# Sparse attention feeding a gated layer: another first stage, another load order

## The chip, the cores and the metric

The kernel runs on one core of a Trainium2 chip. A core has five engines with instruction streams of their own: TensorE (PE, matrix products and transposes into PSUM), VectorE (DVE), ScalarE (ACT), GpSimd (POOL) and SyncE (SP, which here only issues transfers). They meet through semaphores, and each works through its own instructions strictly in order: an instruction that waits holds up all that stand behind it on its engine. Sixteen DMA engines move data between device memory and SBUF. SP, ACT and POOL issue transfers on a queue each (q1, q10 and q0 in the profile). The metric is the device time of one execution in microseconds.

## The reference

Inputs are q, k, v of shape (4, 8, 768, 64), and the weights of a gated layer, w_gate and w_val (512 x 1536) and w_out (1536 x 512).

```
ub[t, c]  = sum over d of max(q[t,d] * kmin[c,d], q[t,d] * kmax[c,d])   # per head; chunks of 32 keys
top       = the 6 chunks with the largest ub, of those not ahead of t's own chunk
scores    = q @ k.T / 8, only where the chunk is in top and the key isn't ahead of t
attn      = softmax(scores)
x         = attn @ v, the heads side by side           # 3072 x 512
out       = (sigmoid(x @ w_gate) * (x @ w_val)) @ w_out
```

The first 128 rows of a sequence have at most four chunks, so there all causal chunks are selected. For the others the selection has to be made. The bound is written as a product: max(q kmin, q kmax) = q kmin + max(q, 0) (kmax - kmin), so that queries and their rectified copy, one below the other in 128 partitions, meet key minima and ranges (kcat) in a single product.

## The kernel before

The work is cut into nine stages. Batch 0 starts with stages of 128 rows (stage 0), 256 rows (stage 1) and 384 rows (stage 2), and the other three batches are two stages of 384 rows each. Every stage has a preparation (queries and keys transposed so that head_dim lies in the partitions; chunk minima and maxima; bounds; selection), the attention (scores, exponentials, product with the values, normalization, transposition to xT), and the gated layer (products with w_gate and w_val called gv, tanh called gate, hglu, and the output product o).

The order of all instructions is written out by hand in a list, ORDER: one name per operation, kind:stage.count, with /1 or /2 for the second or third engine that may do it. The class Plan resolves the names and emits the operations in that order; each engine gets those of its own in the order of the list. Plan also has estimated times, from which it decides only where TensorE gets filler products (fill, line 340: products of zeros, up to 36 us of its estimate) so that its clock stays up while it waits. It knows only the waits of its estimate. PSUM has two large accumulators of two banks ("big") and four small ones of one bank ("m"), handed out in turn: a new one waits until the fourth one before it has been read.

Stage 0 has a form of its own. Keys and queries come as 128 x 512 blocks (first_loads, _groups), are transposed by four fp32 products each (line 561) and evicted from PSUM: keys into firstK, queries raw and rectified into first (evict_queries, line 522, four times on ACT). From the bounds (L699) it takes a guard, a number for each query and head that is subtracted from its scores so that the exponential stays in range (L704 to L708). The guard is transposed and copied into eight extra rows of first (L712), and firstK has minus one there, so that a single product of 72 rows gives guarded scores (L810). After the exponential (L815), GpSimd zeroes what lies ahead of the diagonal (L821). Then the product with the values (L835) and the normalization (L846, L848).

Stages 1 and 2 are made by prep_groups too. They transpose into the large accumulators and evict the queries twice for each half of the partitions, raw and rectified (L522 on ACT, L526 on VectorE): eight evictions in stage 1, twelve in stage 2. Chunk minima and maxima are L571, the key block kcat L580 to L591, key evictions L604, the cast of the queries to 16 bit L537. L733 is the bounds' product, L736 to L757 the selection, L761 its copies into the query block, L810 the scores, L891 the gated layer's products, L901 and L903 its gate, L917 the output product.

Stage 0's values arrive in two halves of 128 KB, one on SP's queue and one on ACT's, are then cast to 16 bit by GpSimd (L491). On ACT's queue the order of issue is stage 0's queries, stage 1's first values (256 KB), stage 0's second half of values. GpSimd issues the weights (w0 to w8, L507 and L509) between the constants that it builds.

## Time and profile before

| | us |
|---|---|
| median of 3 runs | 300.29 |
| lowest and highest | 300.08, 301.04 |
| the profiled execution | 300.8 |
| its span, first to last instruction | 298.8 |
| TensorE busy | 284.5 |
| VectorE, ScalarE, GpSimd busy | 212.4, 203.9, 107.5 |
| filler products on TensorE | 11.2 |
| moved by DMA | 27.99 MB |

Times in the views count from the span's first instruction. In the rows of stretches, behind the length stand the busy time of each engine with the number of its instructions (TensorE, its weight loads, VectorE, ScalarE, GpSimd), then the granted TensorE clock, the mean share of the DMA engines in use, and GB/s. In the rows of the timeline stand start, duration, engine, line, operation, output and inputs; in brackets the idle time ahead of it and what ended that. In the rows of a line, behind the number of instructions stand their shortest, median and longest duration in ns, and the first and last start. In the DMA queues' rows stand packets, MB, and the time that the packets took as a share of 16 engines' time.

### The profile page before, as it was taken

The numbers are of one execution on the slowest core, as the hardware profiler recorded it, in microseconds if no ns is written. First come the engines' busy times: TensorE is split into PE (matmuls) and PEld (weight loads), VectorE is DVE, ScalarE is ACT, GpSimd is POOL, SyncE is SP. The second block draws the span as 40 slices with busy tenths as digits, with TensorE's granted clock in tenths as the row PEclk, the third lists the DMA queues.
The fourth block names the chain that finished last, engine by engine and source line by source line (L and its number), as shares of the span: only waits on it lengthen the run. The fifth ranks groups of instructions, "written<-read, shape, count | busy, mean of one in ns | idle before, by whom it ended". The sixth has DMA issues, their size and how long they took to land.

```text
span 298.8 us, 6823 instructions
## 1 busy us (share of the span) xinstructions
PE 284.5 (95%) x2642; PEld 181.2 (61%) x2642; DVE 212.4 (71%) x581; ACT 203.9 (68%) x299; POOL 107.5 (36%) x175
## 2 busy tenths in 40 slices
PE   6668998999999999999999999999999999999995
PEld 3345983865665566566655656766665676555563
DVE  0688788998999898899988886897875434202431
ACT  3578896899786598887995886999636476331221
POOL 7567703685568143273851104326220101000000
PEclk9999999999999999999999999999999999999999
DMA  7999999999699273575790500006210000021012
GB/s 152 256 218 279 229 171 114 193 149 175 74 215 160 43 141 58 96 63 109 111 85 2 124 0 2 3 3 71 20 70 2 35 2 0 2 103 39 0 70 106
DMA packets 110072, 27.99 MB, mean 94 GB/s; under 512 B 100311, under 2 KB 105525, under 8 KB 110040
## 3 DMA queue, kind: packets, MB, share of 16 engines
q1 hardware_dynamic: 81608, 19.28, 31.5%
q0 software_dynamic: 26720, 7.63, 24.3%
q10 hardware_dynamic: 1712, 0.66, 1.1%
q8 instruction: 20, 0.33, 0.5%
q14 instruction: 12, 0.10, 0.1%
HBM read 28.31 MB, written 6.29 MB: 116 GB/s over the span
## 4 chain that ended last, share of the span: by engine, by line
PE 83%; DVE 8%; DMA 4%; ACT 2%; issue 1%; SPq 1%; DVEq 0%; ACTq 0%
PE m_o L917 21%; PE m_v L891 17%; PE m_g L891 16%; PE big_sc L810 12%; PE m_pv L835 6%; PE big_gv L891 5%; PE m_ub L733 4%; DMA ld_q<-in_q_dram 4%; PE m_xtp L861 2%; ACT Qcat L522 1%; DVE kxn L571 1%; DVE mx L749 1%; PE big_kqT L561 1%; ACT at L815 1%; DVE hglu L903 1%
## 5 line engine op out<-in xcount | busy, mean ns | idle before, releaser
L815 ACT ACTIVATE at<-big_sc 128x1024 f16<-128x1024 f32 (+3 forms) x96 | 84.7, 909 | 17.1 <-PE big_sc L810 11.6
L917 PE MATMUL m_o<-wo,hglu 128*128 128x512 f16 (+1 forms) x300 | 72.0, 370 | 0.0
L821 POOL TENSOR_SCALAR_AFFINE_SELECT at<-at 128x384 f16<-128x384 f16 (+2 forms) x66 | 33.3, 515 | 105.5 <-ACT at L815 101.6
L891 PE MATMUL m_v<-xT,wv 128*128 128x384 f16 (+2 forms) x384 | 71.2, 306 | 0.1
L891 PE MATMUL m_g<-xT,wg 128*128 128x384 f16 (+2 forms) x384 | 70.3, 306 | 0.0
L903 DVE SCALAR_TENSOR_TENSOR hglu<-gate,m_v 128x384 f16<-128x384 f16 (+1 forms) x88 | 44.9, 527 | 19.8 <-PE m_v L891 15.5
L901 ACT ACTIVATE gate<-m_g 128x384 f16<-128x384 f32 (+1 forms) x88 | 40.8, 477 | 24.4 <-PE m_g L891 20.3
L891 PEld LDWEIGHTS <-wg 128*128 128x128 f16 x432 | 38.7, 98 | 23.8 <-issue 4.4
L810 PE MATMUL big_sc<-headQ,headK 89*128 89x128 f16 (+2 forms) x472 | 51.6, 240 | 0.8 <-DVE headQ L761 0.6
L891 PEld LDWEIGHTS <-wv 128*128 128x128 f16 x432 | 38.6, 98 | 20.6 <-issue 0.9
L810 PEld LDWEIGHTS <-headK 89*128 89x128 f16 x472 | 33.4, 97 | 12.7 <-issue 1.1
L917 PEld LDWEIGHTS <-hglu 128*128 128x128 f16 x300 | 27.0, 98 | 22.7 <-issue 1.2
L835 PEld LDWEIGHTS <-at 128*128 128x128 f16 x672 | 30.2, 98 | 12.7 <-issue 1.9
L835 PE MATMUL m_pv<-v,at 128*128 128x65 f16 x672 | 34.0, 194 | 1.1 <-POOL at L821 1.1
L761 POOL COPY headQ<-apT 25x384 f16<-25x384 f16 (+1 forms) x30 | 14.7, 490 | 27.1 <-DVE apT L757 25.6
L672 DVE STREAM_TRANSPOSE Qcat<-ld_qb 64x768 f32<-64x768 f32 x24 | 23.1, 964 | 0.8 <-POOL headQ L537 0.4
L924 ACT ACTIVATE osb<-m_o 128x512 f32<-128x512 f32 (+1 forms) x17 | 9.9, 587 | 18.7 <-PE m_o L917 18.7
L903 DVE SCALAR_TENSOR_TENSOR hglu<-gate,big_gv 128x384 f16<-128x384 f16 x12 | 6.6, 553 | 21.9 <-ACT gate L901 20.7
L848 DVE TENSOR_TENSOR xnat<-m_pv,rz 128x384 f16<-128x384 f32 (+1 forms) x34 | 18.1, 534 | 1.2
L537 POOL CAST headQ<-Qcat 64x1536 f16<-64x1536 f32 (+1 forms) x11 | 15.6, 1419 | 8.8 <-ACT Qcat L522 8.6
L901 ACT ACTIVATE gate<-big_gv 128x384 f16<-128x384 f32 x12 | 5.9, 491 | 17.4 <-PE big_gv L891 17.4
L681 ACT ACTIVATE Qcat<-Qcat 64x1536 f32<-64x1536 f32 x11 | 16.3, 1483 | 0.3
(112 smaller groups left out, 314.4 us busy)
## 6 DMA issues: line engine op xcount, KB each, us to landing
out_dram<-osb SPq DMA_DIRECT2D x23, 256.0 KB, 2.2
ld_kb<-in_k_dram SPq DMA_DIRECT2D x24, 192.0 KB, 4.7
ld_qb<-in_q_dram SPq DMA_DIRECT2D x24, 192.0 KB, 3.8
v<-in_v_dram POOLq DMA_DIRECT2D x21, 128.0 KB, 4.7
ld_k<-in_k_dram SPq DMA_DIRECT2D x6, 256.0 KB, 11.9
wg<-in_moe_w_gate_dram POOLq DMA_DIRECT2D x3, 512.0 KB, 14.7
wv<-in_moe_w_val_dram POOLq DMA_DIRECT2D x3, 512.0 KB, 15.0
wo<-in_moe_w_out_dram POOLq DMA_DIRECT2D x3, 512.0 KB, 24.1
```

Of the source, the lines that this page charges most:

```text
L537: copy(tl(("headQ", s), [89, H, st.n], F16)[0:64, h0:h0 + 4, :], tl(("Qcat", s))[0:64, h0:h0 + 4])
L672: nc.vector.transpose(tl(qd, [128, H, HS])[0:64, h:h + 2].rearrange("p a (c t) -> p a c t", t=CH), tl(("ld", "qb", b, u))[64 * e:64 * e + ...
L681: nc.scalar.activation(dst, src, AF.Relu)
L810: nc.tensor.matmul(ps[:, 128 * o:128 * (o + m)], (hk if s else firstK)[0:rows, h, jl:jl + 128], (tl(("headQ", s)) if s else first)[0:rows, ...
L815: add(at(x + 0.03 * t + 0.01), [("ACT", 0.19 + w * 0.815e-3, lambda sc=sc, a=a, w=w: nc.scalar.activation(tl(a, [128, 1024], F16)[:, 0:w], ...
L821: nc.gpsimd.affine_select(out=dg, in_=dg, compare_op=ALU.is_ge, fill=0.0, base=0, pattern=[[0, nd], [1, 128]], channel_multiplier=-1)
L835: nc.tensor.matmul(pvp[:, ib - q0, h % HP, :], tl(a)[:, 128 * o:128 * o + 128], head_v(b, jb // HB)[:, h, jb % HB, :], start=(jb == 0), st ...
L848: nc.vector.tensor_tensor(dst, pvp[:, :, :, 0:64], r.to_broadcast([128, nb, HP, 64]), ALU.mult)
L891: nc.tensor.matmul(ps(i)[:, n * (fb - f0):n * (fb - f0 + 1)], w16[:, c, 128 * fb:128 * fb + 128], tl(("xT", s, c // 2))[:, c % 2, :], star ...
L901: add(at(x) - EV, [("ACT", 0.18 + 0.81 * el, lambda gate=gate, ps=ps: nc.scalar.activation(tl(gate, [128, G * n], F16), ps(0), AF.Tanh, sc ...
L903: add(at(x) - EV, [("DVE", 0.15 + 1.04 * el, lambda gate=gate, hg=hg, ps=ps: nc.vector.scalar_tensor_tensor(tl(hg, [128, G * n], F16), tl( ...
L917: nc.tensor.matmul(tl(o, [128, N]), tl(("hglu", s, fc // G))[:, c0:c0 + 128], wo16[:, fc, cols], start=(fc == 0), stop=(fc == NFB - 1))
```

## The change

Stage 0: the queries are cast to 16 bit in SBUF (q16) and transposed by 16 products with a 16-bit identity, each of 64 columns into one half of the partitions, so that both halves hold the same queries. VectorE then evicts all 128 partitions in one instruction, whose lower bound is a number per partition (-3e38 in the raw half, 0 in the rectified); ACT needs two. Keys go straight into headK; firstK and the copies from it are gone. The scores are now a sum in PSUM: a product of the identity with a block of minus 60000 ahead of the diagonal (later), the keys' product, and a product of lessk (minus one in a head's row) with the guard (gT16). The selection by GpSimd after the exponential goes away in stage 0.

Stages 1 and 2: keys and queries are transposed into small accumulators. Queries are evicted once, raw; the rectified copy is made from SBUF, in two instructions a stage.

Loads: SP's queue carries keys and queries of stages 0 and 1 in a row, then values. ACT's queue carries the two halves of stage 0's values and stage 1's first values; the written order issues them as is.0 (v00i), is.2 (v10), is.1 (v00h). The casts of the values are on ACT but for one (vs.3, vs.4, vs.5 on ACT, vs.6 on GpSimd). On GpSimd two blocks of constants stand ahead of the first weight, and the second half's pattern between the second and third weight. The whole of ORDER is new, for all nine stages; its start:

```
kch.0 is.0 c.0 c.2 is.2 vn.4 qch.0 c.3 is.1 wst0.0 c.9 c.5/1 vn.5 kch.1 wst1.0 vn.6 w0.0 c.8 kTp:0.0 qch.1 Ap:0.1
c.10/1 kxn:0.0 c.6 kch.2 c.4 vs.4/1 qT:0.0 kxn:0.1 wst2.0 kc:0.0 hk:0.0/1 qT:0.1 qch.2 v.0 c.15 c.7 Qc:0.1/1
Qc:0.0 hk:0.1 qT:1.0 vs.5/1 vn.3 w1.0 ps.0 ubp:0.0 Qc:1.0 ubp:0.1 kTp:1.1 c.11 Ap:0.0 Qc:1.1/1 wst3.0 c.12 kxn:1.2
kTp:1.0 c.14 hk:1.2 hk:1.0/1 wst4.0 qT:1.1 hk:1.3 hk:1.1/1 wst5.0 w2.0 kxn:1.3 Qc:1.3/1 wst6.0 c.13 sc:0.0 kxn:1.1
Qc:1.2/1 sc:0.1 kxn:1.0 hq:1.0 sc:0.2 at:0.0 kc:1.0 rl:1.0/1 pv:0.0 wst7.0 sc:0.3 pv:0.2 pv:0.3 pv:0.1 xn:0.0
hq:1.1 at:0.1 ub:1.0 pl.0 xtp:0.0 ubq:1.0 rl:1.1/1 pv:0.4 pv:0.7 pv:0.6 pv:0.5 kch.3 vs.6 xn:0.1 w3.0 wst8.0
xT:0.0/1 ubq:1.1 xtp:0.1 ub:1.1 mx8:1.0 xT:0.1/1 qch.3 gv:0.0 ...
```

In it kch and qch are key and query loads, is the issues on ACT, wst the weight issues, vs the casts of values, kTp and qT the transposes, Qc and hk evictions, rl the rectified copies, kxn and kc the key block, ub the bounds, sc the scores, at the exponentials, pv the product with values, xT the evictions of the stage's output. vn and w mark arrivals in the plan's estimate and emit nothing.

```
@@ constants, on GpSimd unless said
-        weight_tasks(0, -97)
-        add(-96, [("POOL", 0.55, lambda: make_identity(nc, ident32))], r=[("wst", 0)], w=["id32"])
-        weight_tasks(1, -92, ["id32"])
+        add(-96, [("POOL", 0.55, lambda: make_identity(nc, ident32))], w=["id32"])
+        add(-94, [("POOL", 0.75, _first_stage)], r=["id32"], w=["one"])
+        add(-90, to_any(lambda copy: copy(ident16, ident32), 0.17, 0.3, 0.2), r=["id32"], w=["id16"], port=True)
+        add(-90, [("POOL", 0.4, _later)], w=["later"])
...
@@ stage 0's queries (prep_groups)
+            add(0, to_any(_q16, 0.53, 0.6, 0.38), r=[("qch", s, 0), "id16"], w=["q16"], tiles=[("ld", "q", s)], port=True)
...
+                        for e in range(2):
+                            nc.tensor.matmul(ps[64 * e:64 * e + 64, r], q16[:, c0:c0 + 64], ident16, start=True, stop=True)
...
+                    if eng == "DVE":
+                        nc.vector.tensor_scalar(dst, src, floor, None, ALU.max)
+                    else:
+                        for i, f in enumerate((AF.Copy, AF.Relu)):
+                            nc.scalar.activation(dst[64 * i:64 * i + 64], src[64 * i:64 * i + 64], f)
...
@@ rectified queries of stages 1 and 2 (prep_groups)
+                dst, src = tl(("Qcat", s))[64:128, h0:h0 + 4], tl(("Qcat", s))[0:64, h0:h0 + 4]
+                if eng == "ACT":
+                    nc.scalar.activation(dst, src, AF.Relu)
...
@@ scores (attn_tasks)
+                    if s == 0:
+                        nc.tensor.matmul(ps, ident16, later.rearrange("p (o c) -> p o c", o=1).to_broadcast([128, HU, 128]), start=True, stop=False)
...
+                            nc.tensor.matmul(ps[:, 128 * o:128 * o + 128], hk[0:64, h, 0:128], first[0:64, h, :], start=False, stop=False)
...
+                def _guarded(segs=segs, sc=sc):
+                    for o, h, _, _, _ in segs:
+                        nc.tensor.matmul(tl(sc)[:, 128 * o:128 * o + 128], lessk[:, h, :], gT16, start=False, stop=o == HU - 1)
...
-                if t == 0:
+                if t == 0 and s:
                     def _dg(a=a, nd=nd):
@@ loads: queue, what, when the plan expects it
-    LOADS = (("SP", "k00", 4.8), ("Q2", "q00", 4.8), ("SP", "v00a", 8.0), ("Q2", "v00b", 8.0), ("SP", "k10", 10.1), ("SP", "q10", 11.7),
-             ("SP", "k11", 13.3), ("SP", "q11", 16.0), ("Q2", "v10", 17.4), ("SP", "v11", 23.8),
+    LOADS = (("SP", "k00", 4.8), ("SP", "q00", 6.1), ("SP", "k10", 8.0), ("SP", "q10", 9.4), ("SP", "k11", 10.8), ("SP", "q11", 12.8),
+             ("SP", "v11", 21.2), ("Q2", "v00i", 5.0), ("Q2", "v00h", 5.5), ("Q2", "v10", 13.6), ("SP", "k20", 22.7), ("SP", "q20", 24.2),
...
+    QUEUE = (("w0", 11.7), ("w1", 15.3), ("w2", 19.3), ("p00", 20.4), ("w3", 24.0), ("w4", 28.5), ("w5", 32.6), ("w6", 35.8),
```

More of the change, by code (lines that the diff above doesn't have):

```diff
@@ L18 @@
 LATENCY = {"PE": 0.22, "ACT": 0.08, "DVE": 0.06, "POOL": 0.12, "SP": 3.0, "Q0": 3.0, "Q2": 3.0}
+BEGIN = {"DVE": 0.9, "ACT": 0.8, "POOL": 1.3}
 ORDER = """
[L22 to L24 removed]
@@ L362, in _first_stage @@
         def _first_stage():
+            nc.gpsimd.memset(less, 0.0)
+            nc.gpsimd.affine_select(
+                out=less, in_=less, compare_op=ALU.not_equal, fill=-1.0,
+                base=0, pattern=[[-1, H]], channel_multiplier=1)
             nc.gpsimd.memset(pen4, 0.0)
@@ L380, in const_tasks @@
-        add(-79, [("POOL", 0.95, lambda: _spread(nc.gpsimd, 0, 0))], r=["pat0"], w=[("ps", 0), "issue"])
-        add(-79, [("Q0", 0.8, None)], r=[("ps", 0)], w=[("pl", 0), "hkc00", "lane0"])
-        for n in range(3, 9):
-            weight_tasks(n, -78 + n if n < 7 else 9 + n, ["pat0"])
-        add(9, [("POOL", 1.6, lambda: _pattern(1))], r=[("wst", 8)], w=["pat1"])
+                out=later, in_=later, compare_op=ALU.is_ge, fill=NEG,
+                base=0, pattern=[[1, 128]], channel_multiplier=-1)
@@ L465, in transfer @@
             else:
-                add(p, [("ACT", 0.7, lambda: fn(nc.scalar))], r=list(r), w=[("is",) + tuple(key)], tiles=tiles)
-                add(p, [("Q2", us, None)], r=[("is",) + tuple(key)], w=[key, "lane2"], tiles=tiles)
-        for x, (lane, what, land) in list(enumerate(LOADS))[first:last]:
-            us, lane_at[lane] = land - lane_at[lane], land
+                add(0, [("ACT", 0.7, lambda: fn(nc.scalar))], r=list(r), w=[("is",) + (key if isinstance(key, tuple) else (key,))], tiles=tiles)
@@ L775 @@
     hkeys_of = {}
+    ub_keys0 = []
     def attn_tasks(st, t0, t1):
```

509 lines of the change are left out of this document (265 added, 244 removed), and 2 rows, old and new, of the table LOADS.

## The prediction

> **What bounds the kernel now.** I read the page first: engine shares, the slices, the chain.
>
> ```profile
> PE 284.5 (95%) x2642; PEld 181.2 (61%) x2642; DVE 212.4 (71%) x581; ACT 203.9 (68%) x299; POOL 107.5 (36%) x175
> PE   6668998999999999999999999999999999999995
> DMA  7999999999699273575790500006210000021012
> ```
>
> TensorE is the bound, except in the first slices, and there the DMA engines are full. Next I cut the span into stretches, once for all work and once for line 340, the filler products on zeros:
>
> ```profile
> 0.00:24.40 24.40, 16.48 (x104) 9.09 (x105) 13.63 (x32) 13.68 (x22) 16.55 (x38) 1.00 1.06 213
> 24.40:50.00 25.60, 23.11 (x294) 18.88 (x292) 21.38 (x75) 21.18 (x38) 10.31 (x20) 1.00 1.23 198
> 50.00:250.00 200.00, 199.54 (x1931) 127.25 (x1929) 164.94 (x452) 154.24 (x215) 79.64 (x117) 1.00 0.54 77
> 250.00:295.40 45.40, 45.38 (x319) 26.02 (x316) 11.99 (x23) 14.77 (x26) 1.04 (x3) 1.00 0.11 41
> ...
> 0.00:24.40 24.40, 10.52 (x43) 4.36 (x44) 1.00 1.06 213
> 24.40:50.00 25.60, 0.71 (x4) 0.10 (x1) 1.00 1.23 198
> ```
>
> The first number after each length is TensorE. Useful work up to 24.4 us is 16.48 - 10.52 = 6.0 us, so 18.4 us are lost there; 25.6 - 23.1 + 0.7 = 3.2 us are lost from 24.4 to 50, half a microsecond up to 295.4, and 3.4 us behind the last product. The work on TensorE hardly changes, so the time moves by what is lost before 50 us. The chain in order of time says what holds the start:
>
> ```profile
> 3.02 11.39 DMA ld_q<-in_q_dram
> 14.45 0.67 PE big_qT L561 x4
> 15.79 0.69 DVE Qcat L526
> 17.18 1.21 DVE kxn L571 x2
> ```
>
> It begins with stage 1's first query load, which lands 11.4 us after its issue, at 14.4. It ends, for the start, where stage 0's gated layer begins. The timeline:
>
> ```profile
> 1.51 1.23 ACTq L460 DMA_DIRECT2D ld_v<-in_v_dram  x2
> 17.19 0.62 POOL L491 CAST v<-ld_v 128x512 f16<-128x512 f32 x1 [5.57 <-DMA ld_v<-in_v_dram]
> 19.37 1.25 POOL L821 TENSOR_SCALAR_AFFINE_SELECT at<-at 128x512 f16<-128x512 f16 x2
> 20.68 0.33 PE L835 MATMUL m_pv<-v,at 128*128 128x65 f16 x5 [1.10 <-POOL at L821]
> 24.56 1.06 PE L891 MATMUL m_g<-xT,wg 128*128 128x128 f16 x16
> 25.55 0.64 PE L733 MATMUL m_ub<-Qcat,kcat 128*32 128x256 f32 x8
> 26.80 0.44 PE L810 MATMUL big_sc<-headQ,headK 89*128 89x128 f16 x4
> ```
>
> POOL stands 5.57 us behind the half of stage 0's values that ACT's queue brings last, and stage 0's masking (L821) and value products (L835) stand behind that.
>
> **The change part by part.** *Load order.* SP's queue now carries keys and queries of stages 0 and 1, six in a row, ahead of any values. Before, 128 KB of stage 0's values in 256-byte packets stood between stage 0's keys and the loads of stage 1. What these transfers cost is read from the packets of each queue (q0 weights, q1 SP, q10 ACT), here from 4 to 6 us and from 12 to 16 us, with the first transposes of stage 0 and of stage 1:
>
> ```profile
> q10 hardware_dynamic: 760, 0.19, 65.4%
> q0 software_dynamic: 114, 0.12, 34.9%
> ...
> q0 software_dynamic: 399, 0.39, 57.7%
> q1 hardware_dynamic: 394, 0.72, 54.3%
> ...
> 5.94 1.09 PE L561 MATMUL m_kT<-ident,ld_k 128*128 128x128 f32 x4 [1.48 <-POOL ident masks.py:199]
> 12.80 0.66 PE L561 MATMUL big_kT<-ident,ld_k 128*128 128x128 f32 x4 [1.36 <-DMA ld_k<-in_k_dram]
> ```
>
> q0 and q1 get the same number of packets, 25 per engine in 4 us: one packet of each queue per 0.16 us. A 256 KB key or query load is 128 packets of 2 KB, 8 per engine, so 1.3 us each. Stage 0's keys are transposed at 5.9 us now; five more loads of 1.3 us end near 12.5; the last but one of them is stage 1's second key load, near 11. The chain's present head, stage 1's queries at 14.4, comes some 4 us earlier (the third of the five, near 10). That would be the gain, were it not for the next item.
>
> *Values on ACT's queue.* It carries halves v00i and v00h (128 KB each, stage 0) and v10 (256 KB, stage 1). The written order issues them as is.0, is.2, is.1: v00h goes last, behind v10. The kernel before does the same with its own last half:
>
> ```profile
> ld_v<-in_v_dram ACTq DMA_DIRECT2D x1, 256.0 KB, 10.1
> ld_v<-in_v_dram ACTq DMA_DIRECT2D x1, 128.0 KB, 14.9
> ...
> 1.32 0.89 POOL L507 DMA_DIRECT2D wg<-in_moe_w_gate_dram  x1 [0.81 <-POOLq L990]
> 2.74 0.78 POOL L507 DMA_DIRECT2D wv<-in_moe_w_val_dram  x1
> 4.46 0.76 POOL L507 DMA_DIRECT2D wg<-in_moe_w_gate_dram  x1
> ```
>
> Issued at 1.51 and 2.1, they land at 11.6 and 17.0; that is POOL's wait above. Now the cast of v00h stands on ACT (vs.5/1), ahead of everything ACT does for stage 1. Call its landing X. The distance of those two landings, 5.4 us, is 32 packets per engine at 0.16 us. What lies ahead of it now is 128 KB of small packets in place of 256 KB of queries in large ones (no dearer: 760 small packets went in 2 us), and the weights' first packets come later, because two constant blocks of POOL now stand before the first weight issue (they lie in the gaps of 0.5 and 0.9 us between the three issues above; 1.3 together, less what stays behind). That lets up to 1.3 us x 24 packets per engine and us (760 in 2 us), some 30, pass without competition, worth 30 x 0.12 = 3.6 us. So v10 lands between 8.0 and 11.6; X is 5.1 to 5.4 later, and up to 1 us more because the third queue now holds 2 KB packets all the time: 13.1 to 18. No row is nearer to one end; I take 15.0.
>
> *What waits behind X.* On ACT in order: the cast, an eviction (Qc:1.1), then, because the transposes kTp:1.0 need the bank that this eviction frees, one hand-over to TensorE, two key evictions, two query evictions, the exponential of stage 0, a rectifying copy, the second exponential, the second copy, two evictions of stage 0's outputs. Rows:
>
> ```profile
> 22.98 0.64 PE L733 MATMUL m_ub<-Qcat,kcat 128*32 128x256 f32 x8
> L522 ACT ACTIVATE Qcat<-big_qT x6: 615/620/626, 15.1 to 21.2; 64x512 f32<-64x512 f32 x6
> L604 ACT CAST headK<-big_kT x2: 735/738/740, 22.9 to 24.3; 64x512 f16<-64x512 f32 x2
> L815 ACT ACTIVATE at<-m_sc x2: 597/597/597, 16.7 to 18.0; 128x512 f16<-128x512 f32 x2
> 24.87 1.03 ACT L537 CAST headQ<-Qcat 64x1024 f16<-64x1024 f32 x1
> 23.50 0.74 ACT L866 COPY xT<-m_xtp 128x256 f16<-128x256 f16 x2
> ```
>
> The cast of 128x256 has no row; 0.37 (half the last one) to 0.62 (POOL's 128x512), I take 0.4. The rectifying copy from SBUF has none either; the cast of 64x1024 on ACT, 1.03, is nearest, 0.62 (half as large) and 1.48 (the page's 64x1536) bound it. The hand-over is the four transposes of 0.66 and a little: 0.8. Sum: 0.4 + 0.62 + 0.8 + 2 x 0.74 + 2 x 0.62 + 0.60 + 1.03 + 0.60 + 1.03 + 0.74 = 8.5, and ten hand-overs of 0.03: 8.9. VectorE's two reductions (L571) and its key block run beside it and end at about X + 6, when the first bound product is due. So the gated layer starts at X + 8.9 = 23.9 against 24.4 to 24.6 now; its last bound product (L733) comes at X + 8.1 = 23.1 against 25.55; the first score product of stage 1 (3.8 us behind the first bound product, as 26.80 is behind 22.98, and a little for a normalization that stands between) at about X + 10.5 = 25.5 against 26.80. The gated layer leads by 0.6, the scores by 1.3, the bounds by 2.4; TensorE loses less by something between the first two: 1.0 us. Each microsecond of X is a microsecond of this; it is even near X = 16.
>
> *Guard, mask and 16-bit queries of stage 0.* Added on TensorE: 2 mask products of 512 columns, 8 guard products, 16 products of 64 columns for 4 transposes; removed: 2 selects on POOL (1.25) and 2 copies of stage 0's keys on ACT. All of it lies before 24.4 us, where 18.4 us of TensorE are empty or filler; cost nothing, and the sum above already has stage 0 without its selects. If X were early, gT16, now behind four VectorE operations of 0.7 us, would be next.
>
> *Rectified queries from SBUF.* Stage 2 had twelve evictions of 0.63, now six and two copies:
>
> ```profile
> L522 ACT ACTIVATE Qcat<-big_kqT x11: 622/629/639, 33.6 to 45.1; 64x512 f32<-64x512 f32 x11
> L681 ACT ACTIVATE Qcat<-Qcat 64x1536 f32<-64x1536 f32 x11 | 16.3, 1483 | 0.3
> ```
>
> 12 x 0.63 - 6 x 0.63 - 2 x 1.48 = 0.8 us less on ACT and VectorE. Of the 3.2 us lost between 24.4 and 50 I give it half of that, 0.4; bounds 0 and 0.8.
>
> *Weights.* The issue of the third piece moves behind the second half's pattern, from 4.5 to about 8 us. The DMA engines are full and move the same bytes; three microseconds on a piece that is needed after 24 us cost nothing, unless X is early.
>
> *The order of stages 3 to 8* is written anew. The half microsecond lost there now bounds the gain; a loss has no row. Taken as 0.
>
> Sum: 1.0 + 0.4 = 1.4 us. The profiled execution took 300.8 us (span 298.8 and 2.0 around it): 299.4. It lies 0.5 above the median of 300.29: **298.9 us**.
>
> **The rivals.** *Slower: the values are late.* X at 17.5 or later puts the gated layer at 26.4 and the scores at 28.0; some 2 us lost, 302.3 by the median. [...] It decides from X = 16.5 on. [...] Chance 0.25.
>
> *Faster: the values are hidden.* If X is 12 or less, stage 1's second key load (near 11) leads: two groups of transposes, then the same ACT work from its key evictions on (7.0 of the 8.9), the gated layer near 20.5, some 4 us early. The third weight piece, issued 3.5 us later than now, would then be waited for; I leave 3.0 us less lost: 297.3. For it: small packets go at 380 per us while nothing competes. Chance 0.18.
>
> *TensorE cold.* From about 13 us to X + 1.1 it has nothing to do and, since the order's planner expects no wait there, probably no filler. Four transposes took 1.09 us at 5.94 and 0.66 at 12.80. If the gap makes them slow again, two groups of transposes and the score products pay 0.4 each: 1.0 us, 299.9, no change. [...] Chance 0.12.
>
> *Slower: banks and order.* Transposed keys and queries of stages 1 and 2 now take four small accumulators, shared with the gated layer, each held for four evictions of 0.6 to 0.7. A TensorE that waits for two of them, or one slip in the rewritten later stages, costs 2 us net of the gain: 301.7. Against it: those stages lose almost nothing now with equal rules. Chance 0.10.
>
> **How the numbers follow.** Forecast (X from 13 to 16) 0.35; late 0.25, hidden 0.18, cold 0.12, banks 0.10. About 0.3%, 0.9 us, is what a measurement here can tell from no change. Faster: 0.25 of the forecast's 0.35 (its part with X below 15.4) and 0.18, and 0.02 of the rest: 0.45. Same: 0.10 and most of the cold case: 0.20. Slower: 0.35. The likeliest case alone runs from 297.8 to 300.0; the range over all, 296.5 to 302.8, leaves out less than the outer half of the hidden and the late case.
>
> **What would show it.** In the changed profile: stage 1's keys and queries landing at 8 to 13 us; one wait of ACT for ld_v, 2 to 5 us long, ending at X; TensorE idle over the same stretch; gated layer at X + 8.9; no L821 of 128x512; the loss up to 50 us near 20. Wrong if ACT's wait is absent or ends after 16.5, if the banks make new waits between 25 and 45 us, or if TensorE is no longer full after 50.

## The result and the profile after

| | before | after |
|---|---|---|
| median, us | 300.19 | 308.60 |
| lowest and highest | 300.08, 301.04 | 307.95, 311.67 |
| profiled execution, and its span | 300.8, 298.8 | 308.58, 306.8 |
| mean granted clock of TensorE | 1.000 | 0.976 |

The change is slower: the ratio is 1.0287 [1.025, 1.0323], some 8.4 us, where 298.9 was forecast and 302.8 was the upper end. The page of the kernel after (engine shares, the slices, the granted clock in tenths):

```profile
PE 288.0 (94%) x2647; PEld 181.9 (59%) x2647; DVE 215.9 (70%) x584; ACT 190.2 (62%) x280; POOL 115.2 (38%) x184
PE   6599879859999999999999999998999999999995
PEclk9859999989999999999999999999999999999999
```

Two things are new. The clock has two dips, one in slices 2 and 3 and one in the ninth, and TensorE has a hole of its own in the eighth and ninth. Now the stretches of the kernel after, all work first (TensorE is the first number behind the length), then the filler products alone:

```profile
0.00:24.40 24.40, 18.46 (x136) 10.46 (x137) 17.22 (x48) 11.94 (x20) 17.45 (x39) 0.79 1.06 219
24.40:50.00 25.60, 22.39 (x275) 17.88 (x273) 21.11 (x72) 19.66 (x34) 11.29 (x21) 1.00 1.28 193
50.00:80.00 30.00, 25.73 (x292) 17.36 (x290) 22.45 (x59) 21.82 (x28) 15.73 (x22) 0.94 1.10 157
80.00:250.00 170.00, 168.08 (x1586) 105.25 (x1583) 136.35 (x373) 121.08 (x174) 69.09 (x101) 1.00 0.44 62
...
0.00:24.40 24.40, 6.89 (x26) 2.88 (x26) 0.79 1.06 219
24.40:50.00 25.60, 0.60 (x2) 0.11 (x2) 1.00 1.28 193
```

The same cut of the kernel before, where the prediction had 50 to 250 us in one row:

```profile
50.00:80.00 30.00, 29.62 (x331) 19.97 (x329) 27.20 (x88) 25.73 (x34) 17.76 (x27) 1.00 1.06 152
80.00:250.00 170.00, 169.93 (x1602) 107.28 (x1601) 137.74 (x365) 128.51 (x182) 61.88 (x91) 1.00 0.45 63
```

TensorE's time without work of its own (idle or filler), before and after: up to 24.4 us 18.4 and 24.4 - (18.46 - 6.89) = 12.8; from 24.4 to 50 us 3.2 and 25.6 - 22.39 + 0.60 = 3.8; from 50 to 80 us 0.4 and 4.3; from 80 to 250 us 0.1 and 1.9; the tail of 3.4 is the same. Together it is 25.5 and 26.3. The rest of the 8.0 us of span is TensorE's own work, without filler: 284.5 - 11.2 = 273.3 before, 288.0 - 7.5 = 280.5 after. So 7.2 us are work that takes longer (slow clock, added products), although 5.6 us less were lost at the start. Part of that 5.6 is no gain, since a product stretched by a slow clock counts as work here (four fp32 transposes took 0.66 us at 11.73, and 1.08 at 13.28, where the clock was 0.50).

The start, in the timeline of the kernel after:

```profile
9.32 0.41 ACT L496 CAST v<-ld_v 128x256 f16<-128x256 f32 x1
11.73 0.66 PE L573 MATMUL m_kT<-ident,ld_k 128*128 128x128 f32 x4 [0.60 <-DMA ld_k<-in_k_dram]
12.42 0.69 DVE L578 TENSOR_REDUCE kxn<-m_kT 128x32 f32<-128x512 f32 x1 [0.23 <-PE m_kT L573]
17.19 1.78 DVE L601 TENSOR_TENSOR kcat<-kxn,kmx 64x64 f32<-64x64 f32 x1
17.78 1.05 POOL L551 CAST headQ<-Qcat 64x1024 f16<-64x1024 f32 x1
19.92 1.08 PE L768 MATMUL m_ub<-Qcat,kcat 128*32 128x256 f32 x8 [0.21 <-DVE kcat L603]
23.36 1.07 PE L937 MATMUL m_g<-xT,wg 128*128 128x128 f16 x16
```

ACT casts the second half of stage 0's values at 9.32 and did not wait for it: the row has no bracket. The loads that ACT issues in the first 4 us (count, KB each, median us to landing) explain that:

```profile
ld_v<-in_v_dram ACTq DMA_DIRECT2D x2, 128.0 KB, 6.5
ld_v<-in_v_dram ACTq DMA_DIRECT2D x1, 256.0 KB, 5.3
```

The half in question was issued at 1.81 and landed 6.5 us later, at 8.3. The late wait is gone altogether. What then leads is VectorE. It works without a gap from 12.42 to 19.77 and releases the first bound product at 19.92. One operation in that chain, L601 (a minimum; the expectation of s_ord calls it a subtraction), takes 1.78 us beside a cast by GpSimd from 17.78 to 18.83.

The clock, by stretches of 1 us around both ends of the first dip, and around the second (the clock is the third number from the end):

```profile
12.00:13.00 1.00, 1.00 (x9) 0.89 (x7) 0.75 (x2) 0.32 (x1) 0.92 (x4) 0.71 1.21 210
13.00:14.00 1.00, 1.00 (x6) 0.71 (x4) 0.99 (x3) 0.57 (x1) 1.00 (x2) 0.50 1.20 193
22.00:23.00 1.00, 1.00 (x13) 0.82 (x15) 0.96 (x10) 0.10 (x1) 0.00 (x0) 0.67 1.15 277
...
63.00:67.00 4.00, 0.54 (x5) 0.21 (x4) 3.19 (x3) 1.49 (x2) 2.06 (x3) 1.00 1.18 187
67.00:70.00 3.00, 3.00 (x26) 2.17 (x25) 2.97 (x4) 0.98 (x2) 2.80 (x4) 0.50 1.22 193
```

From the shares of the first and the last row, the clock is at half from 12.42 to 22.66, 10.2 us. The second dip, to 70.4, lasts 3.4 us and follows 4 us in which TensorE worked for 0.54. In the two dips TensorE had 6.9 and 3.4 us of work without filler; if all of it ran at half speed, 5.2 us of that are the clock's.

The row hides one thing: ahead of its first fall the clock stands at 1.00 in the rows of the kernel after, of h1, e_hk and e_vn, although the first products of the kernel after ran slowly. Four key transposes took 1.08 us at 4.49 and 0.66 at 11.73.

The hole ahead of the second dip, in the timeline of the kernel after:

```profile
55.27 1.76 POOL L455 DMA_DIRECT2D v<-in_v_dram  x2
63.77 0.98 DVE L678 STREAM_TRANSPOSE kT_kT<-ld_kb 128x768 f32<-128x768 f32 x1 [3.85 <-DMA ld_kb<-in_k_dram]
64.82 1.46 POOL L698 CAST headK<-kT_kT 64x1536 f16<-64x1536 f32 x1 [5.77 <-DVE kT_kT L678]
66.33 1.06 POOL L796 COPY headQ<-apT 25x384 f16<-25x384 f16 x2
66.89 0.81 PE L850 MATMUL big_sc<-headQ,headK 89*128 89x128 f16 x6 [3.46 <-POOL headQ L796]
```

VectorE stands 3.85 us for a key block of stage 3. GpSimd's cast of those keys stands 5.77 us, and stage 2's mask copies (L796) stand behind it in GpSimd's order although their input is ready; TensorE waits 3.46 us for them. In the kernel before, the values of stage 3 are issued later and the same transposition has no wait:

```profile
60.06 0.89 POOL L441 DMA_DIRECT2D v<-in_v_dram  x1
61.69 0.97 DVE L641 STREAM_TRANSPOSE kT_kT<-ld_kb 128x768 f32<-128x768 f32 x1
```

Stage 3's key blocks issued from 53 to 59 us took 3.4 us to land (the median of four) in the kernel before, and beside the values 6.3 in the kernel after:

```profile
ld_kb<-in_k_dram SPq DMA_DIRECT2D x4, 192.0 KB, 3.4
...
ld_kb<-in_k_dram SPq DMA_DIRECT2D x4, 192.0 KB, 6.3
```

### The profile page after: what moved, and what is told of

Its sections match the earlier page's. It is cut to its first block, busy times and chain, and to the rows that moved or that the text cites. A ratio compares the mean times of both kernels' runs of the same rounds, so it can differ in the third digit from the quotient of the medians.

```text
span 306.8 us, 6829 instructions
## 1 busy us (share of the span) xinstructions
PE 288.0 (94%) x2647; PEld 181.9 (59%) x2647; DVE 215.9 (70%) x584; ACT 190.2 (62%) x280; POOL 115.2 (38%) x184
## 4 chain that ended last, share of the span: by engine, by line
PE 83%; DVE 6%; DMA 5%; ACT 2%; SPq 2%; issue 1%; POOL 1%; DVEq 0%; POOLq 0%; ACTq 0%
PE m_o L963 19%; PE m_g L937 17%; PE m_v L937 17%; PE big_sc L850 11%; PE m_pv L881 6%; PE big_gv L937 5%; PE m_ub L768 4%; DMA ld_k<-in_k_dram 3%; DMA ld_kb<-in_k_dram 2%; PE m_xtp L907 2%; DVE kxn L578 2%; ACT at L861 1%; SPq L472 1%; SPq L436 1%; DVE kcat L601 1%
## 5 line engine op out<-in xcount | busy, mean ns | idle before, releaser
L861 ACT ACTIVATE at<-big_sc 128x896 f16<-128x896 f32 (+3 forms) x96 | 85.5, 908 | 26.3 <-PE big_sc L850 20.0
L963 PE MATMUL m_o<-wo,hglu 128*128 128x512 f16 (+1 forms) x300 | 74.0, 373 | 1.0 <-DVE hglu L949 1.0
L867 POOL TENSOR_SCALAR_AFFINE_SELECT at<-at 128x384 f16<-128x384 f16 (+1 forms) x64 | 32.3, 516 | 98.1 <-ACT at L861 78.7
L881 PE MATMUL m_pv<-v,at 128*128 128x65 f16 x672 | 34.7, 195 | 1.9 <-DVE hglu L949 0.8
L796 POOL COPY headQ<-apT 25x384 f16<-25x384 f16 (+1 forms) x40 | 19.5, 486 | 34.5 <-DVE apT L792 30.7
L698 POOL CAST headK<-kT_kT 64x1536 f16<-64x1536 f32 x10 | 14.6, 1459 | 8.3 <-DVE kT_kT L678 7.8
L455 POOL DMA_DIRECT2D v<-in_v_dram x18 | 16.6, 925 | 0.3 <-PE m_v L937 0.3
```

Source lines behind the costliest of these rows:

```text
L455: nc.gpsimd.dma_start(dst[:, :, i, :], v[b, :, r0 + 128 * i:r0 + 128 * i + 128].rearrange("h p d -> p h d"))
L796: copy(tl(("headQ", s), [89, H, st.n], F16)[64:89, h, :], tl(apT)[32 * i:32 * i + 25, :])
L861: add(at(x + 0.03 * t + 0.01), [("ACT", 0.19 + w * 0.815e-3, lambda sc=sc, a=a, w=w: nc.scalar.activation(tl(a, [128, 1024], F16)[:, 0:w], ...
L867: nc.gpsimd.affine_select(out=dg, in_=dg, compare_op=ALU.is_ge, fill=0.0, base=0, pattern=[[0, nd], [1, 128]], channel_multiplier=-1)
L881: nc.tensor.matmul(pvp[:, ib - q0, h % HP, :], tl(a)[:, 128 * o:128 * o + 128], head_v(b, jb // HB)[:, h, jb % HB, :], start=(jb == 0), st ...
L963: nc.tensor.matmul(tl(o, [128, N]), tl(("hglu", s, fc // G))[:, c0:c0 + 128], wo16[:, fc, cols], start=(fc == 0), stop=(fc == NFB - 1))
```

## The experiments

Two theories stood first. *The later order*: the loss is made from stage 3 on, in the hole between 60 and 71 us and behind it. *The start*: stage 0 and 1, with TensorE's clock at half for 10.2 us and behind VectorE's chain, put everything else late. In the diffs ORDER's names stand as in the kernels; a name with a minus is taken away at its place, one with a plus put in there.

**Exchange of the order at stage 3.** h1 has the instructions and the start of the kernel after, and from Qct:3.0 on (stage 3's first query transposition, near 54 us) the relative order of the kernel before. h2 is the reverse. An order also names the engine of some operations (/1, /2), so some change their engine with it.

```
h1:   ... at:2.9 gv:1.4           # the order after, to here
    - Qct:3.0 at:2.4 ...          # the order after, from here
    + gate:1.2 gv:1.5 ...         # what is left, in the order before
h2:   the same cut, the order before first, then the order after
```

> The changed kernel with its written order kept up to stage 3's first query transpose (Qct:3.0, at about 54 us), and from there on the operations that are left in the relative order of the kernel before. Nothing else changes. Theory 1, the time was lost in the rewritten order of the later stages: TensorE idled 6.2 us behind 50 us and ran some 4 us at half its clock (about 1.8 us), against 0.5 us idle before; 7.5 us of this comes back, so 301.1 by the median of 308.6. Theory 2, the start itself is what lost (colder clock, later weights, and the stalls behind are its echo): 306 or more.

> The reverse: the kernel before with its own order up to stage 3's first query transpose (Qct:3.0), and from there on what is left in the relative order of the changed kernel. Theory 1 (the later order loses): 300.2 + 7.5 = 307.7, with TensorE waiting for the mask copies near 64 us. Theory 2 (the start loses): 300 to 301.

h1: 303.18, ratio 1.0075 [1.0054, 1.0096]. h2: 305.98, 1.0171 [1.0154, 1.0188]. Each time lies between the values that the two theories gave. The parts add up to 2.46% of the 2.87%. From 60 to 75 us, h1 and then h2, with the wait of h2:

```profile
60.00:75.00 15.00, 14.62 (x202) 9.74 (x202) 14.35 (x29) 13.76 (x16) 11.04 (x15) 1.00 1.26 171
```

```profile
60.00:75.00 15.00, 11.41 (x128) 6.66 (x127) 11.90 (x32) 10.41 (x12) 7.79 (x11) 0.89 1.31 181
65.44 0.55 PE L808 MATMUL big_sc<-headQ,headK 89*128 89x128 f16 x6 [3.59 <-POOL headQ L759]
```

The hole and the slow clock behind it go with the later order, whatever the start is. By the two ratios the later order costs 5.1 us (h2) to 6.4 (after less h1), the start 2.3 (h1) to 3.5 (after less h2).

**What makes the hole.** e_hk takes GpSimd's cast of the keys out of the way of the mask copies. e_vn issues stage 3's values later, so that they do not move beside the key blocks. e_both does both.

```
e_hk:  o:0.1 kn:3.0 - hk:3.0 ... o:0.4 mq:2.7 + hk:3.0
e_vn:  pv:2.2 - vn:3.0 qb:3.4 ... pv:2.3 - vn:3.1 ... o:0.4 + vn:3.0 ... osb:1.1 + vn:3.1
e_both: the two together
```

> The changed kernel with one operation moved: GpSimd's first cast of stage 3's keys (hk:3.0) goes from ahead of stage 2's last mask copies (mq:2.6, mq:2.5, mq:2.7) to behind them. Theory 1a, TensorE stood 3.46 us at 66.89 because these copies stood on GpSimd behind a cast that waits for late key blocks: the wait goes and with it the cold clock behind it (1.8 us), about 5 us, 303.5; the key blocks land as late as they did, at 63.7. Theory 1b, VectorE's transpose of the late key blocks (its 3.85 us wait at 63.77) holds TensorE just as well: 307 or more, with a wait for VectorE at the same place.

> The changed kernel with the first two of stage 3's value loads (vn:3.0, vn:3.1) issued on GpSimd's queue some 6 us later, as in the kernel before (there at 60.1 and 62.6; in the changed kernel at 55.3 and 56.2). Theory 1c, their small packets slowed stage 3's second set of key blocks (landing 6 to 7.3 us behind the issue instead of 3.4): the last block lands at 61.0 instead of 63.65, the wait of 3.46 us shrinks to about 1, the clock stays up: 308.6 - 2.6 - 1.8 = 304.2. If the key blocks are late for another reason (output or query blocks on SP's own queue): they land near 63.6 again, and 308 to 309.

> The changed kernel with both single moves of the first experiments: stage 3's first value loads later, and GpSimd's cast of stage 3's keys behind the mask copies. If the stall near 65 us is the late key blocks and the cast ahead of the copies together, the 1.3 us that were left with the loads moved go as well: 306.04 - 1.3 = 304.7. If VectorE's transposes of the key blocks hold the same work: 305.7 to 306.3, with a wait for VectorE near 68 us.

e_hk: 308.64, 1.0266 [1.0222, 1.0311], nothing gained by the median; its executions lie far apart (306.98 to 310.31), and the profiled one is the fastest. e_vn: 306.04, 1.0182 [1.0165, 1.02], some 2.6 us gained (3.2 by the ratios), between the two values expected. e_both: 307.51, 1.0238 [1.0198, 1.0278], slower than both values expected. The key blocks and the wait in e_vn, then the wait in e_hk:

```profile
ld_kb<-in_k_dram SPq DMA_DIRECT2D x4, 192.0 KB, 4.5
...
65.15 0.55 PE L847 MATMUL big_sc<-headQ,headK 89*128 89x128 f16 x6 [1.29 <-POOL headQ L793]
```

```profile
68.75 1.62 PE L765 MATMUL m_ub<-Qcat,kcat 128*32 128x384 f32 x8 [1.44 <-DVE kcat L689]
```

With the values out of the way the blocks land in 4.5 us, not 6.3, and TensorE's wait falls from 3.46 to 1.29: the collision is a part of the hole, worth about half of what the later order costs. With the cast out of the way TensorE waits 2 us later for stage 3's bounds, whose key block is late for the same transposition, and e_both still waits for that key block twice, 0.99 and 0.48 us near 68.2.

From 60 to 75 us TensorE works for 11.54 us in the kernel after, and for 13.71 (e_vn), 13.56 (e_hk) and 13.53 (e_both) in these executions, there at full clock. So in the traces each move shrinks the hole alike, and the two together shrink it no further. Why the medians of e_hk and e_both don't follow, the traces don't show: e_hk's slower executions have none.

**The reverse, in the kernel before.** b_vn issues stage 3's values early in the kernel before.

```
o:1.6 + vn:3.0 vn:3.1 at:2.10 ... sc:2.5 - vn:3.0 ... o:1.0 - vn:3.1
```

> The kernel before (300.6) with stage 3's first two value loads issued early on GpSimd's queue, right behind the eighth key block's issue, as the changed kernel does. Collision alone: the second set of key blocks lands 2 to 4 us later than the 61.3 of before; since the mask copies of stage 2 stand ahead of VectorE's transposes and of the cast in this order, TensorE has work meanwhile, and the time stays within 0.5 of 300.6. If late key blocks cost by themselves: 302 to 304.

300.64, 0.9989 [0.9966, 1.0012]. The loads were issued from 58.26 on only, since GpSimd stands behind an exponential there (2.12 us at 55.81), and VectorE had the last block at 60.97. The collision hardly came about, so this says nothing on it.

**A later cut.** h3 keeps the order after up to sc:3.2 (near 80 us), then the order before.

> The changed kernel with its own order up to stage 3's first scores (sc:3.2, at about 80 us), and from there on the rest in the relative order of the kernel before. It splits the 5.4 us that the later order costs (308.6 - 303.2). In the changed kernel's profile the stretch from 54 to 80 us holds 3.9 us more idle time and about 1.8 us of slow clock, the stretches behind it 1.9 us of idle time against 0.2. If the stall near 65 us is the larger part: 308.6 - 1.7 = 306.9. If the later stages hold most of it: 304.5 or less.

308.62, 1.0257 [1.0228, 1.0285], slower than both values expected. Behind 80 us the idle time falls from 1.9 to 0.2 us, but the hole was longer in this one:

```profile
68.30 0.55 PE L847 MATMUL big_sc<-headQ,headK 89*128 89x128 f16 x6 [4.74 <-POOL headQ L793]
```

So the order behind 80 us costs something in the kernel after, but this run doesn't separate how much.

**The start: the clock.** From h1 on, with the later order out of the way. s_warm adds filler products ahead of four operations of stages 0 and 1, where the plan expects no wait.

```
+FILLS = {'qT:1.0': 2.8, 'kTp:1.1': 0.95, 'sc:0.0': 1.6, 'ub:1.0': 1.9}
...
+            elif eng == "PE" and self.tasks[i][5] and self.kinds[i][1][1:] in FILLS:
+                out.append((None, (FILLS[self.kinds[i][1][1:]], self.tasks[i][5], tiles[0] in new)))
```

> The kernel with the changed start and the old later order (h1, 303.2), with more products on zeros on TensorE ahead of four operations where it stood idle: nine instead of three ahead of stage 1's first query transpose (qT:1.0), some ahead of its second key transpose (kTp:1.1), stage 0's first scores (sc:0.0) and stage 1's first bounds (ub:1.0). Theory 3, the start loses because TensorE's clock is halved for some 7 us between 12 and 25 us: the granted clock stays at 1 up to 24.4, about 3.3 us of slower products go, the gated layer starts near 23 instead of 24.4, and the time is 301.5 or less. Rival 3b, VectorE's chain to stage 1's key block (ready at 20.2) sets the start whatever the clock: the clock is up, the gated layer starts within 0.5 us of 24.4, 302.7 to 303.5.

302.14, 1.0053 [1.0035, 1.0072], between 0.7 and 1.0 us better than h1. The two intervals overlap, so the gain is likely but not clear of noise.

```profile
0.00:24.40 24.40, 18.83 (x149) 10.30 (x150) 15.85 (x46) 11.94 (x19) 17.17 (x38) 0.93 1.06 218
23.89 1.07 PE L938 MATMUL m_g<-xT,wg 128*128 128x128 f16 x16
```

The clock over the start goes from 0.86 in h1 to 0.93, and the gated layer begins 0.5 us earlier (h1: 24.40). The row understates the difference: four transposes still took 1.11 us at 10.33 and 1.06 at 12.91 in h1, where the row stands at 1.00, and 0.60 at 11.84 in s_warm. The clock looks like a part of the start's price, not all of it.

**The start: VectorE's chain.** s_hk gives two key evictions to ACT. s_ord moves rectified copies ahead of the exponentials, a cast from GpSimd to ACT and the product with the values ahead of the bounds. s_port is s_ord with filler products as in s_warm (1.0 us instead of 1.9 ahead of ub:1.0).

```
s_hk:  - hk:1.2 + hk:1.2/1 ... - hk:1.3 + hk:1.3/1
s_ord: sc:0.1 kxn:1.0 hq:1.0 + rl:1.0/1 sc:0.2 at:0.0 kc:1.0 - rl:1.0/1 + vs.6 pv:0.0 ...
       xn:0.0 - hq:1.1 + rl:1.1/1 at:0.1 + hq:1.1/1 pv:0.4 pv:0.7 pv:0.6 pv:0.5 xn:0.1 ub:1.0 ...
```

> The same kernel (h1, 303.2) with two of stage 1's key evictions (hk:1.2, hk:1.3), 0.73 us each on VectorE, given to ACT. By rival 3b VectorE's chain to the key block is 1.5 us shorter, the first bounds come some 1 us earlier, 302.2. By theory 3 (the clock) little: TensorE is the slow one, 302.9 to 303.5; ACT gets later, which may cost up to 0.5.

> The kernel with the changed start and the old later order (h1, 303.2), with five moves inside the start: the rectified copies (rl:1.0, rl:1.1) go ahead of the exponentials on ACT, the second query cast (hq:1.1) from GpSimd to ACT, the cast of stage 1's first values (vs.6) ahead of it, and on TensorE stage 0's second half of value products and its normalization (pv:0.4 to pv:0.7, xn:0.1) ahead of stage 1's first bounds, which wait for VectorE's key block. Theory 3c, the start loses because VectorE's chain to the key block is slowed by GpSimd's casts (one subtraction took 1.78 us) and because stage 0's work stands behind the bounds: key block near 18.3 instead of 20, gated layer 1.5 us earlier, 301.7. If only the clock matters: 303 or so, with the clock still halved between 12 and 25 us.

> The same five moves together with the additional products on zeros (as in s_warm, fewer ahead of the bounds). If clock and order each cost something of their own: 303.2 - 1.0 - 1.5 = 300.7, no slower than the kernel before; if they are the same loss seen twice: 301.7 to 302.2.

s_hk: 305.17, 1.0152 [1.0092, 1.0213], a miss: the first bound product came at 21.49, later than before the move. s_ord: 303.83, 1.0097 [1.0073, 1.012], no gain; its clock was 0.53 from 12 to 24.4 us. s_port: 302.66, 1.0071 [1.0043, 1.01], no better than h1, although it did what it was meant to:

```profile
17.07 0.61 POOL L497 CAST v<-ld_v 128x512 f16<-128x512 f32 x1
17.24 0.56 DVE L602 TENSOR_TENSOR kcat<-kxn,kmx 64x64 f32<-64x64 f32 x1
22.80 1.07 PE L938 MATMUL m_g<-xT,wg 128*128 128x128 f16 x16
24.40:50.00 25.60, 21.30 (x261) 17.14 (x259) 20.78 (x70) 18.84 (x33) 11.45 (x21) 1.00 1.28 194
50.00:297.10 247.10, 246.24 (x2245) 153.23 (x2243) 175.76 (x470) 167.58 (x240) 77.92 (x114) 1.00 0.45 70
```

Beside a shorter cast by GpSimd, that of the values (0.61 us, not 1.05), the minimum takes 0.56 us, not 1.78; the clock is full once the first products are through (transposes of 1.05 us at 4.93 and 0.65 at 10.63); the gated layer begins 1.8 us earlier than before. But hardly more work is done by 24.4 us: 21.30 - 0.4 (filler) + 246.24 = 267.1 us are left, and 23.11 - 0.71 + 244.92 = 267.3 in the kernel before. From 24.4 to 50 us TensorE then loses 25.6 - 21.30 + 0.4 = 4.7 us, against 3.2 before, and at 50 us more work is left (246.24 against 244.92, below). TensorE's waits in that stretch, the three about stage 2's first transposes:

```profile
31.39 0.63 PE L646 MATMUL m_qT<-ident,ld_q 128*128 128x128 f32 x4 [0.49 <-PE m_pv L882]
32.73 0.57 PE L882 MATMUL m_pv<-v,at 128*128 128x65 f16 x13 [0.71 <-ACT Qcat L653]
33.86 0.66 PE L646 MATMUL m_qT<-ident,ld_q 128*128 128x128 f32 x4 [0.56 <-ACT Qcat L653]
```

They are waits of products in small accumulators, two of them for ACT's eviction of stage 2's queries, 1.8 us together; the kernel before has one of 0.21 us among its transposes of stage 2 (38.93), and both have one more of 1.4 to 1.6 us at stage 2's bounds.

**The start: weights and the second stretch.** The weights' pieces 4 to 6 land later in the kernel after (29.0, 33.0, 37.0 us) than before (23.6, 29.0, 34.0). s_w is s_warm with the first four issues earlier. h5 is s_warm with the order before from the first gated layer's product on, and the small accumulators kept.

```
s_w:  - wst0.0 ... qch.0 + wst0.0 c.3 ... + wst1.0 is.1 ... (wst2.0, wst3.0 alike)
h5:   ... xT:0.1/1 qch.3          # the order after, to here; then the order before
```

> The kernel with the changed start, the old later order and more products on zeros (s_warm, 302.1), with GpSimd's first four weight issues moved ahead of the constants that stand before them (the first two as early as in the kernel before, the third ahead of the rows of the second half's mask block, the fourth ahead of the pattern's spread). If late weights hold the remaining 1.6 us: pieces four to six land 2 us earlier (27, 31, 35 us) and the time falls by 0.8 to 1.6, to 300.5 to 301.3. If not: 301.8 to 302.5, or up to 1 more where stage 1's keys get later.

> The same kernel (s_warm, 302.1) with its own order only up to the first gated-layer product (gv:0.0), and from there on the relative order of the kernel before; an operation that finds no free accumulator is taken later, because stage 2 still uses the small ones. If the rewritten order between 24 and 54 us holds the remaining 1.6 us: 300.5 to 301.3. If it is the small accumulators or the load order: 302 or more, and more than 303 where the old order and the small accumulators hinder each other.

s_w: 303.72, 1.0104 [1.0058, 1.0149]; the move did not do what it was meant to. The first two issues stayed at 2.40 and 3.28, the next two came at 6.12 and 10.97 for 6.90 and 11.34, and the pieces landed at 29.4, 33.5 and 37.4, no earlier. So the weights were not tested. TensorE waits for weights once in the kernel after, 0.22 us ahead of a weight load at 37.03, and once in s_port, 0.29 us. h5: 305.66, 1.0148 [1.0105, 1.0191]: the order before does not fit the small accumulators (waits of 1.92 and 0.94 us for ACT's key evictions).

**The start alone, in the kernel before.** The decisive test of the prediction's premise: b_is exchanges two issues on ACT's queue of the kernel before, so that the half of stage 0's values goes ahead of stage 1's.

```
- is.2 ... - is.1
+ is.1 ... + is.2
```

> The kernel before (300.6) with one exchange on ACT's queue: stage 0's second half of values is issued ahead of stage 1's first values. By the prediction's mechanism (GpSimd stood 5.57 us behind that half, the masking and the value products behind it) the half lands near 12 instead of 17, the wait of 1.10 us of TensorE at 20.68 goes, the gated layer starts up to 1 us earlier, and the time falls by 0.5 to 1.0: 299.6 to 300.1. If an earlier start of the gated layer is lost again behind it, as in the changed kernel: 300.3 to 300.9.

301.15, 1.0009 [0.9986, 1.0031]: no change. Its timeline and stretches, and the last stretch of the kernel before:

```profile
11.66 0.62 POOL L489 CAST v<-ld_v 128x512 f16<-128x512 f32 x1
23.07 1.06 PE L889 MATMUL m_g<-xT,wg 128*128 128x128 f16 x16
56.83 0.89 POOL L439 DMA_DIRECT2D v<-in_v_dram  x1
62.90 0.98 DVE L639 STREAM_TRANSPOSE kT_kT<-ld_kb 128x768 f32<-128x768 f32 x1 [3.80 <-DMA ld_kb<-in_k_dram]
69.33 1.18 PE L731 MATMUL m_ub<-Qcat,kcat 128*32 128x384 f32 x8 [2.38 <-DVE kcat L653]
...
70.00:75.00 5.00, 5.00 (x72) 3.60 (x66) 4.18 (x21) 2.87 (x3) 1.46 (x1) 0.66 1.20 190
50.00:296.00 246.00, 243.50 (x2227) 152.91 (x2224) 173.88 (x470) 167.45 (x238) 78.96 (x116) 0.99 0.46 70
```

```profile
50.00:295.40 245.40, 244.92 (x2248) 153.27 (x2245) 176.93 (x475) 169.01 (x241) 80.68 (x118) 1.00 0.46 70
```

GpSimd's wait of 5.57 us is gone, the gated layer begins 1.5 us earlier, and at 50 us 1.4 us less work is left. Then the whole of it is lost: the values of stage 3 move up with everything else on GpSimd (56.83 for 60.06), the key blocks are issued no earlier (from 53.49, before from 53.08) and take 4.8 us where they took 3.4, VectorE waits 3.80 us for one, TensorE waits 2.38, and its clock is halved for 3.4 us behind that (0.66 over 5 us). It is a hole like that of the kernel after, and only the start was changed.

b_v moves the values' issues of b_is behind GpSimd's cast hk:3.0, away from the key blocks. b_vk also puts stage 3's second set of key blocks ahead of its first query blocks on SP's queue.

```
b_v:  sc:2.5 - vn:3.0 ... o:1.0 - vn:3.1 ... pv:2.16 hk:3.0 + vn:3.0 vn:3.1
b_vk: - qb:3.0 + kb:3.4 ... - qb:3.1 + kb:3.5 ...  - kb:3.4 + qb:3.0 ...  (and kTt:3.0 ahead of Qct:3.0; Qct, rl, hq:3.0 later)
```

> The kernel before with the exchange on ACT's queue (b_is, 301.15 against 300.89) and stage 3's first two value loads issued behind GpSimd's cast of stage 3's keys, about 10 us later. If the gain of the earlier start (1.4 us less work left at 50 us) was eaten by these loads colliding with the key blocks: the last key block lands near 60.5 instead of 62.8, TensorE's wait of 2.38 us at 69.3 shrinks below 0.5, and the time is 299.5 (0.9953 of before). If the key blocks set the time whatever runs beside them (their issue did not move with the start: 53.5 against 53.1): 300.5 to 301.

> The same kernel with stage 3's second set of key blocks issued ahead of its first set of query blocks on SP's queue, and VectorE's transposes in the matching order. If stage 3's key block is what the start runs into: the keys are complete some 4 us earlier, near 57, TensorE does not wait near 69 us, and the time is 299.5 or less. If the query blocks, now last, take the keys' place: 300.5 to 301.5, with a wait for the rectified queries near 69.

b_v: 299.36 beside 299.70 for the kernel before on the same chip, 0.9987 [0.9974, 1.0]. b_vk: 303.92, 1.0116 [1.007, 1.0162], with a wait of 3.31 us for an exponential at 68.40. The wait in b_v:

```profile
67.69 1.53 PE L731 MATMUL m_ub<-Qcat,kcat 128*32 128x384 f32 x8 [0.81 <-DVE kcat L653]
```

With the values behind the keys, 2.38 us become 0.81. That is the best version here, but its interval reaches to no change and overlaps that of b_is, so it is not shown that some of the earlier start is kept.

## Why the prediction was wrong

**The premise failed:** "The work on TensorE hardly changes, so the time moves by what is lost before 50 us." That loss fell from 18.4 + 3.2 to 12.8 + 3.8, by 5.0 us, and the time rose by 8.4. TensorE's work did change, from 273.3 to 280.5 us, and up to 3.5 us of the fall are only work of the start (6.9 us of it) drawn out by half the clock. b_is is the same point without any other change: 1.5 us earlier at the start, none at the end. The reading that fits b_is and b_v is that the stream of key blocks sets a time of its own near 61 us, and that TensorE's fullness behind 50 us in the kernel before only meant that nothing arrived there too early.

**The largest wrong term was the order of stages 3 to 8, "Taken as 0".** It costs 5.1 to 6.4 us, by h1 and h2. The reason given, that those stages lose almost nothing now, was about the order that the change replaces. A view that could have warned was there: stage 3's values, issued by GpSimd at 60.06, follow close on the key blocks, the last of which lands at 61.28, and a GpSimd that is freed of selects and waits comes to them sooner. That collision is a part of the hole (e_vn). For the rest no run stands alone: the waits speak for an order in which VectorE reaches the transposition before its block is there and GpSimd's cast holds up the mask copies.

**X was put at 15.0 (13.1 to 18); it was 8.3.** The packets of the small loads were costed against a weights queue that is full from the start. In the kernel after the queues' rows of the first 6 us have SP's and ACT's alone (294 and 1949 packets), though the weights are issued from 2.39 on, and ACT's three loads landed 5.3 to 6.5 us behind their issue. So the late rival's condition never came. The hidden rival's did, but not its gain: the gated layer began at 23.36 in this execution (20.5 was given), and at 24.40, 24.00, 24.72, 24.56 and 24.57 in the profiled executions of h1, e_vn, e_hk, e_both and h3, which have the same start; before it was 24.56. Where the clock is halved within the start differs between these executions (12.4 to 22.7 us here, 17.5 to 24.3 in h1), so a single one of them is no measure of the start.

**The chain behind the loads was summed on the wrong engine.** The sum went over ACT; VectorE's two reductions and its key block, said to run beside it, were in truth the lead. Second keys at 11.73, VectorE full to 19.77, bounds at 19.92, the gated layer 11.6 us behind the keys where the hidden rival had 9.5. Part of that is a minimum of 1.78 us (L601) that takes 0.56 in s_port, beside a shorter cast, and 0.69 in the kernel before (L589 at 18.75), beside none.

**The cold rival was right in kind, wrong in place and price.** It gave 1.0 us for a gap ending at X + 1.1. TensorE had no wait for the values; its gap ahead of stage 1's first transposes, 8.75 to 10.29, was for their queries. The clock fell all the same, for 10.2 us, and once more for 3.4 us behind the hole, which no rival had. With a full clock in s_port TensorE's own work is 275.9 us (287.1 busy, 11.2 filler) against 280.5 in the kernel after, so by that comparison, whose later order is another, slow running costs some 4.6 us of the 7.2; from the two dips alone it is at most 5.2.

**Weights, guard and mask at nothing:** the one wait for weights that shows on TensorE is 0.22 us. The added products are in the 275.9 - 273.3 = 2.6 us of further work; most of it lies in the start's empty time, as was said, but neither they nor the rectified copies (0.4 us of gain) were run alone, and the loss from 24.4 to 50 us did not fall, so the 0.4 was not found. The bank rival's waits, TensorE for small accumulators, are there and small: 0.98 us at 15.35 and 0.47 at 33.29 in the kernel after, 1.8 in s_port near 32; they are not the cause of the 8.4.

**What stays open.** Of the start's 2.3 to 3.5 us, the clock seems to be 0.7 to 1.0 (s_warm, not clear of noise). With a full clock and an early gated layer s_port still loses 1.5 us more than the kernel before between 24.4 and 50 us. Its waits near 32 us are of that size and speak for the small accumulators, but no run took them away alone (h5, which came nearest, changed the order too).

## What to carry to other kernels

A full TensorE behind some point is no proof that an earlier start is worth its length: find the next time that the DMA stream sets by itself (here the last key block near 61 us), and ask what would reach it early. Work that moves up brings its own transfers along (b_is: stage 3's values at 56.83 for 60.06); a load that gains nothing by being early is better kept behind the one that is awaited (b_v: a wait of 0.81 us for 2.38). When an order is written anew, cost the new order at its known tight places and leave room for a loss there, and sum the start's chain on each engine, not only on the one that waits now.

## What the runs showed of the hardware

*The clock at half, with TensorE partly in use ahead of it.* By the shares of the rows the clock stood at half for 10.2 and 3.4 us in the kernel after, for 6.8 in h1 and for 3.4 in b_is; the two longer stretches are near to three and two times the shortest. In the 3.4 us, the shortest of these lengths, ahead of a fall TensorE was busy for 1.5 us at the start of the kernel after (from 9.01), for 0.1 in its hole, for 1.4 in b_is, where the gap was only 2.38 us, and for 2.1 in h1 (from 14.05). What sets the fall and its length, no run shows.

*VectorE's work on the key block beside GpSimd's casts.* The minimum of two 64x64 blocks took 1.78 us from 17.19 beside a cast from 17.78 to 18.83 (kernel after, L601), and 0.56 from 17.24 beside one from 17.07 to 17.68 (s_port, L602). The two end 0.14 and 0.12 us behind the cast. Beside an issue of weights and no cast it took 0.69 in the kernel before (L589 at 18.75), and the subtraction of the same shape 0.27 in the kernel after (L603 at 19.50). The row of 1.78 us opens 0.59 us ahead of the cast, and no run moved the cast alone: what stretches the minimum stays open.

*Small transfers beside each other.* Key blocks of 192 KB took 3.4 us to land in the kernel before, 4.3 in b_v and 4.5 in e_vn, with no values beside them, 4.8 beside those of b_is, and 6.3 beside two value loads of 128 KB on GpSimd's queue (medians of four).
